# Values of the first group requested ahead of the weights, second-layer weights in another row order, probabilities as 24 rows

## The chip, the cores and the metric

The kernel runs on one core of a Trainium2 chip. The time is the device time of one launch in microseconds (us). A core has a matrix engine (PE, with its weight loads PEld), a vector engine (DVE), an activation engine (ACT), GpSimd (POOL) and a sync engine (SP). DMA requests are issued by SP, ACT and POOL; only POOL's may change the type on the way (fp32 in memory, fp16 on the chip).

## The reference

Attention over 4 batches, 8 heads, 768 positions and 64 values a head. Heads 0, 2 and 6 see all earlier positions ("retrieval" heads); the other five see the first 4 positions and a window of 64. The result, as a matrix x of 3072 rows by 512, goes through four experts, each with two layers, and their outputs are summed with normalised probabilities:

```
scores = scale * np.matmul(q, k.transpose(0, 1, 3, 2))
scores = np.where(mask[None, :, :, :], scores, -1000000000.0)
a = np.exp(scores - np.max(scores, axis=-1, keepdims=True))
a = a / (np.sum(a, axis=-1, keepdims=True) + 1e-09)
attn_out = np.matmul(a, v)
...
p = domain_probs / (domain_probs.sum(-1, keepdims=True) + 1e-09)
for e in range(E):
    h = np.maximum(x @ w1[e], 0.0)
    out += p[:, e:e + 1] * (h @ w2[e])
```

w1[e] is 512 by 1024 and w2[e] is 1024 by 512, in fp32: 2 MB each, 16 MB for the four experts.

## The kernel before

The order of instructions on every engine is fixed when the program is built: the code is emitted in the order in which each engine is to run it, attention interleaved with the experts by planned durations.

Attention works on groups of 384 positions (8 groups, two a batch). Group 0 comes first and has PE for itself. Its queries and keys come as fp32 by SP's and ACT's queues (L384, L397), and its values by POOL's queue, which casts them to fp16 (`load_v`, L287): head 0 at L406, heads 2, 1, 3, 4, 6 at L477, heads 5 and 7 at L479. Between these two stands `load_w1(0)` (L478), the first-layer weights of expert 0, in two requests of 64 partitions; `load_w2(0)` (L480) follows. Streaming heads land in `vS`, retrieval heads in `vR`. Masks are added on PE from `bC` and `bS`, which POOL builds (L423 to L449); the third column block of `bS` is a copy made by ACT (L812). A matmul on the tile `warm` (L416, `warm_up`) computes nothing that is used; it is put in where PE would wait. For the values of heads 3, 4, 5, 6 and 7 there are 4, 4, 6, 8 and 10 of them (L748, L680). Values are multiplied at L691 (retrieval) and L755 (streaming); the normalised result goes through ACT (L773, L783), DVE (L778) or a transpose (L732, L736) into `xT`.

The first four tiles of 128 rows go through the experts plainly (`plain_steps`, L956): first for three tiles, expert by expert, then for the fourth. Layer one is L969 (weights `w1sb` stationary, `xT` moving, 384 columns, or 128 columns for the fourth tile), the relu is ACT L982 into `hA`, layer two is L990 (`hA` stationary, `w2sb` moving, 512 columns), and DVE adds up (L1002, L1006). DVE also forms sums of the second-layer weights (`weight_sums`, L940) into `tsb`. The other 20 tiles go in pairs (`pair_steps`, L1068): layer one at L1081 (256 columns, `w1sb` stationary) and layer two at L1114 as seven products of half size.

The row order of the weights matters here. A hidden row of the second layer has to sit on the partition on which its hidden unit sits in `hA`. `load_w2` (L331) puts row 8*fi + fo of w2 on partition fi: eight neighbouring rows, 16 KB in one stretch of memory for each partition. The hidden units of one block of 128 are then every eighth column of w1, and `w1_tile` (L327) reads the stationary operand with a step of eight fp16 elements.

POOL's queue of requests is paced by hand with `landed` (L487): a copy of one element that waits for a request to land. In order: `load_w1(1)`, wait for w1(0), keys and queries of group 1, wait for w2(0), `load_w2(1)`, wait for the queries, retrieval values of group 1, `load_w1(2)`, wait for w2(1), and so on (L497 to L512).

The probabilities are read once at L398 as `[128, 24, 4]` in pieces of 16 bytes, normalised on DVE in `small_things` (L884 to L894) and, at the start of expert 1, transposed on PE (`turn_probs`, L900, L902), copied by DVE (L906) and written to a table `p_rows` in memory (L907), from which `load_probs` (L1028) reads two rows at a time for the pairs. The first four tiles use the normalised tile `p_sb` directly (L999).

Of the kernel before, what the change touches and what calls it, by code (L numbers as in the profile page):

```python
# [17 lines left out]
def kernel(  # L18
# [34 lines left out]
    P = 128  # L53
# [83 lines left out]
    mW = mS.rearrange("p t x -> p (t x)")[:, 0 : (WT + 2) * WQ].rearrange(  # L137
        "p (t x) -> p t x", t=WT + 2
    )
    probs = pers.tile([P, NTILE, E], FP32, name="probs")  # L140
    psums = pers.tile([P, NTILE], FP32, name="psums")
    rprobs = pers.tile([P, NTILE], FP32, name="rprobs")
    p_sb = pers.tile([P, NTILE, E], FP32, name="p_sb")

# [177 lines left out]
                in_=x[u, :, :, f0:f1],  # L324
            )

    def w1_tile(e, ct, ft):  # L327

        return w1sb[:, e * DMP + ct, :].rearrange("p (x f) -> p f x", f=FTP)[:, ft, :]

    def load_w2(e):  # L331
        gp.dma_start(
            out=w2sb[:, e * FTP : (e + 1) * FTP, :],
            in_=moe_w2[e].rearrange("(fi fo) d -> fi fo d", fi=P),
        )


# [38 lines left out]

    q32, k32 = rows32(0), rows32(1)
    v_s32 = early[0:NS, 0:1024].bitcast(FP32).rearrange("p (h d) -> p h d", h=H)
    for h in range(H):
        if h == 2:  # L380
            nc.sync.dma_start(
                out=v_s32, in_=v[0, :, 0:NS, :].rearrange("h r d -> r h d")
            )
        nc.sync.dma_start(out=k32[:, :, h, :], in_=rows_of(k, 0, h, 0))  # L384
        if h == HP:

            nc.scalar.add_instruction(
                mybir.InstLoadActFuncSet(
                    name=nc.get_next_instruction_name(),
                    engine=ENG.Activation,  # L390
                    act_func_set_id=[x.name for x in SETS].index(
                        "natural_log_exp_and_others"
                    ),
                )
            )
        eng = nc.scalar if h < HP else nc.sync
        eng.dma_start(out=q32[:, :, h, :], in_=rows_of(q, 0, h, 0))  # L397
    nc.sync.dma_start(  # L398
        out=probs, in_=moe_domain_probs.rearrange("(t p) e -> p t e", p=P)
    )  # L400
    nc.vector.memset(warm.bitcast(FP32), 0.0)
    nc.vector.memset(eps, 1e-9)
# [71 lines left out]

    mask_c(bC, 0.0, -60000.0)
    mask_s(bS[:, 0:2, :], 2, 0.0, -60000.0)
    load_v(0, 0, [2, 1, 3, 4, 6])  # L477
    load_w1(0, 0, F)  # L478
    load_v(0, 0, [5, 7])  # L479
    load_w2(0)  # L480
    zero(gp, kR[0][:, 1, :, :, :])
    zero(gp, kS[:, 1, :, :, :])
# [41 lines left out]
    def attention(b, c):  # L524
# [151 lines left out]
        def values_r(h):  # L676

            ps = pV.tile([P, 512], FP32, name="pV", bufs=2)
            if first:
                warm_up(ps, {6: 8}.get(h, 0), 256)  # L680
            ps = ps[:, 0 : 3 * (D + 2)].rearrange("p (j x) -> p j x", j=3)
            work = []
            for j in range(3):
                for es, parts in es_of[h]:
                    for t, o, q0, nq in parts:
                        x = j * P - q0
                        if 0 <= x < nq:
                            work.append((j, t, es[:, o + x : o + x + P]))
            ns = 0
            for n, (j, t, lhsT) in enumerate(work):  # L690
                nc.tensor.matmul(  # L691
                    out=ps[:, j, 0 : D + 1],
                    lhsT=lhsT,
                    rhs=vR[i][:, t, RH.index(h), 0 : D + 1],
                    start=(n == 0),
                    stop=(n == len(work) - 1),
                    skip_group_check=True,
                )
                ns += mm_ns(D + 1)
                if ns > 200 and n < len(work) - 1:  # L700
                    yield ns
                    ns = 0
            rs = att.tile([P, 3, 1], FP32, name="rs", bufs=2)
            nc.vector.tensor_scalar(
                out=rs, in0=ps[:, :, D : D + 1], scalar1=1e-9, scalar2=None,
                op0=ALU.add,
            )
            nc.vector.reciprocal(out=rs, in_=rs)
            ct, u = PLACE[h]
            x = x_pair if ct else x_one  # L710
            nc.vector.tensor_tensor(
                out=x[:, :, half(u)], in0=ps[:, :, 0:D],
                in1=rs.to_broadcast([P, 3, D]), op=ALU.mult,
            )
            yield ns
            if h != 2 and not first:
                nc.sync.dma_start(
                    out=xT[g][:, ct, :].rearrange("p (j x) -> p j x", j=3),
                    in_=x.rearrange("p j x -> p (j x)"),
                    transpose=True,  # L720
                )
# [16 lines left out]
        def values(h):  # L738
            if RETR[h]:
                yield from values_r(h)  # L740
                return
            ct, u = PLACE[h]
            if first and u == 1:
                ps = pO.tile([P, 512], FP32, name="pO", bufs=2)
            else:
                ps = pV.tile([P, 512], FP32, name="pV", bufs=2)
            if first:
                warm_up(ps, {3: 4, 4: 4, 5: 6, 7: 10}.get(h, 0), 256)  # L748
            work = []
            for es, parts in es_of[h]:  # L750
                for t, o, q0, nq in parts:
                    work.append((es, t, o, q0, nq))
            ns = 0
            for n, (es, t, o, q0, nq) in enumerate(work):
                nc.tensor.matmul(  # L755
                    out=ps[:, q0 : q0 + nq],
                    lhsT=v_tile(b, c, h, t),
                    rhs=es[:, o : o + nq],
                    start=(n == 0),
                    stop=(n == len(work) - 1),  # L760
                    skip_group_check=True,
                )
                ns += mm_ns(nq)
                if ns > 300 and n < len(work) - 1:
                    yield ns
                    ns = 0

            r, o = half(u), half(1 - u)
            pair = first and h in (3, 4)
            if not pair or u == 0:  # L770
                rc_of[0] = att.tile([P, CH], FP32, name="rc", bufs=2)
            rc = rc_of[0]
            nc.scalar.activation(  # L773
                out=rc[r, :], in_=ps[o, 0:CH], func=AF.Ln, bias=eps[o, :]
            )

            def scale(r=r, ps=ps):
                nc.vector.tensor_tensor(  # L778
                    out=xT[g][r, ct, :], in0=ps[r, 0:CH], in1=rc[r, :], op=ALU.mult
                )  # L780

            if not pair:
                nc.scalar.activation(out=rc[r, :], in_=rc[r, :], func=AF.Exp, scale=-1.0)  # L783
                later(scale, g)
            elif u == 0:
                scale_of[0] = scale
            else:
                nc.scalar.activation(out=rc, in_=rc, func=AF.Exp, scale=-1.0)
                later(scale_of[0], g)
                later(scale, g)  # L790

            yield ns + (600.0 if g == 1 else 400.0)
# [14 lines left out]
        if first:  # L807
# [1 line left out]
            yield from scores(0)  # L809
            sink_row(1)  # L810
            sink_row(3)
            nc.scalar.copy(out=bS[:, 2, :], in_=bS[:, 1, :])  # L812
            yield from transposes(1)
            yield from scores(2)
            sink_row(4)
# [59 lines left out]
    def small_things():  # L875
        def to_mask(x, bias):
# [4 lines left out]
        to_mask(mC, bC)  # L881
        to_mask(mS[:, 0:3, :], bS)
        to_mask(mS[:, 3, :], bS[:, 2, :])
        nc.vector.tensor_reduce(  # L884
            out=psums, in_=probs, axis=mybir.AxisListType.X, op=ALU.add
        )
        nc.vector.tensor_scalar(
            out=psums, in0=psums, scalar1=1e-9, scalar2=None, op0=ALU.add
        )
        nc.vector.reciprocal(out=rprobs, in_=psums)  # L890
        for e in range(E):
            nc.vector.tensor_tensor(
                out=p_sb[:, :, e], in0=probs[:, :, e], in1=rprobs, op=ALU.mult
            )  # L894


    p_rows = tc.dram_tile([NTILE, E * P], FP32, name="p_rows")
    pair0 = 4

    def turn_probs():  # L900
        ps = bank()
        nc.tensor.transpose(  # L902
            ps[0 : NTILE * E, 0:P], p_sb.rearrange("p t e -> p (t e)"), ident32
        )
        pT = moe.tile([P, P], FP32, name="pT", tag="sums", bufs=1)[0 : NTILE * E, :]
        nc.vector.tensor_copy(out=pT, in_=ps[0 : NTILE * E, 0:P])  # L906
        nc.sync.dma_start(out=p_rows.rearrange("t (e x) -> (t e) x", e=E), in_=pT)  # L907


    behind = []  # L910
# [45 lines left out]
    def plain_steps(nt0, tiles, e, tokens, n0):  # L956
# [6 lines left out]
        for f0 in [0, *range(ahead, FTP)]:  # L963
# [3 lines left out]
            def layer1(ft, n):  # L967
                ct = cts[n]
                nc.tensor.matmul(  # L969
                    out=pss[ft][:, 0:cols_n],  # L970
                    lhsT=w1_tile(e, ct, ft),
                    rhs=x[:, ct, :],
                    start=(n == 0),
                    stop=(n == DMP - 1),
# [93 lines left out]
    def pair_steps(nt0, nxt):  # L1068

        sums = [lambda: last_weight_sum(E - 1)] if nt0 == pair0 else []  # L1070
        for e in range(E):
# [5 lines left out]
            for f0 in range(0, FTP, 2):  # L1077
                ps = bank()
                for f in range(2):
                    for ct in range(DMP):  # L1080
                        nc.tensor.matmul(  # L1081
                            out=ps[:, f * PC : (f + 1) * PC],
                            lhsT=w1_tile(e, ct, f0 + f),
                            rhs=xs[:, ct, :],
                            start=(ct == 0),
                            stop=(ct == DMP - 1),
# [98 lines left out]
    def moe_steps():  # L1185
        for e in range(E):
            if e == 1:
                turn_probs()
            yield from plain_steps(0, 3, e, lambda: xT[0], (e % 2) * FTP * CH)
            weight_sums(e)  # L1190
        for e in range(E):
# [121 lines left out]
```

## Time and profile before

| | us |
|---|---|
| median of 4 runs | 386.55 (386.44 to 387.88) |
| the profiled execution | 386.31 |
| its span, first to last instruction | 384.6 |
| PE busy | 376.5 (98%) |
| PEld busy | 334.5 (87%) |
| DVE busy | 235.3 (61%) |
| ACT busy | 234.4 (61%) |
| POOL busy | 110.5 (29%) |

The busy shares are averages over the whole span; the kernel has stages with different limits. Group 0's attention fills about the first 22.6 us, the plain steps reach to about 91 us, the pairs fill the rest. In the lists, xN is a count of instructions, "idle" is the time in which the engine had nothing to run just before, and an arrow names what ended it. A line of the chain gives start, length, engine, tile and line of the work that the end waited for.

### The profile page before, as it was taken

Reading aid. Unit: us, or ns where it says so; the run is one execution under the profiler, and the core shown is the slowest. Engines: PE = TensorE matmul, PEld = TensorE weight load, DVE = VectorE, ACT = ScalarE, POOL = GpSimd, SP = SyncE. Lnnn points to the kernel's source line nnn. Section 1 sums busy time; section 2 is a strip of 40 time slices with the busy share of each in tenths; the row PEclk is TensorE's granted clock in tenths of the full one; section 3 lists DMA queues with packets and bytes.
Section 4 is the critical chain, followed back from the end, with each engine's and each line's share of the span. In section 5 each row is a group of like instructions: output and inputs, shape, how many; then the busy total and the mean of one; then the engine's idle time right before and its main releaser. Section 6 shows DMA issues by size and latency. Waiting matters only on the chain.

```text
span 384.6 us, 9369 instructions
## 1 busy us (share of the span) xinstructions
PE 376.5 (98%) x3814; PEld 334.5 (87%) x3814; DVE 235.3 (61%) x516; ACT 234.4 (61%) x476; POOL 110.5 (29%) x152
## 2 busy tenths in 40 slices
PE   7989999999999999999999999999999999999996
PEld 4776567678998998999998998999998999999995
DVE  6745787567766657766547566775556565355440
ACT  3863568657786876765765775764765684551630
POOL 8823534855138028213800118202100000000000
PEclk9999999999999999999999999999999999999999
DMA  8999999999499959965950669965510210110001
GB/s 165 164 208 204 185 185 185 129 175 151 71 132 128 127 96 96 145 125 48 141 78 16 113 116 76 145 129 41 80 56 13 68 57 2 56 55 30 29 0 56
DMA packets 123608, 39.19 MB, mean 102 GB/s; under 512 B 116232, under 2 KB 116780, under 8 KB 123052
## 3 DMA queue, kind: packets, MB, share of 16 engines
q0 software_dynamic: 83232, 19.01, 55.8%
q1 hardware_dynamic: 38732, 19.18, 22.4%
q8 instruction: 30, 0.49, 0.6%
q10 hardware_dynamic: 1600, 0.39, 0.5%
q14 instruction: 14, 0.11, 0.1%
HBM read 44.88 MB, written 6.34 MB: 133 GB/s over the span
## 4 chain that ended last, share of the span: by engine, by line
PE 92%; POOL 3%; DMA 2%; DVE 1%; ACT 1%; issue 0%; POOLq 0%; ACTq 0%
PE pA L1081 37%; PE pO L1114 32%; PE pA L969 7%; PE pO L990 7%; PE pA L643 5%; DMA vS<-in_v_dram 2%; PE pV L691 2%; PE pV L755 2%; POOL vR L291 1%; POOL vS L297 1%; ACT es L661 1%; POOL early L440 0%; POOL w1sb L322 0%; PE pO L416 0%; PE pV L545 0%
## 5 line engine op out<-in xcount | busy, mean ns | idle before, releaser
L1081 PE MATMUL pA<-xs,w1sb 128*128 128x256 f16 x1280 | 149.5, 274 | 0.0
L1081 PEld LDWEIGHTS <-w1sb 128*128 128x128 f16 x1280 | 140.1, 145 | 0.6 <-DVE xs L1047 0.3
L1090 ACT ACTIVATE hA<-pA 128x512 f16<-128x512 f32 x160 | 94.6, 597 | 40.3 <-PE pA L1081 37.3
L1114 PEld LDWEIGHTS <-hA 128*128 128x128 f16 x1120 | 106.6, 98 | 12.8
L661 ACT ACTIVATE es<-pA 128x384 f16<-128x384 f32 (+2 forms) x122 | 59.3, 510 | 31.9 <-PE pA L643 27.3
L1114 PE MATMUL pO<-w2sb,hA 128*128 128x256 f16 x640 | 77.8, 272 | 0.0
L293 POOL DMA_DIRECT2D vS<-in_v_dram x30 | 29.6, 988 | 126.2 <-PE pV L755 125.2
L1047 DVE TENSOR_TENSOR xs<-xT,pB 128x1024 f16<-128x1024 f16 (+1 forms) x52 | 49.6, 972 | 20.2 <-PE pA L1081 20.2
L1114 PE MATMUL pO<-tsb,hA 128*128 128x256 f16 x480 | 58.6, 272 | 0.0
L938 DVE TENSOR_TENSOR hA<-hA 128x1024 f16<-128x1024 f16 (+1 forms) x80 | 41.9, 553 | 1.1
L778 DVE TENSOR_TENSOR xT<-pV,rc 64x384 f16<-64x384 f32 x37 | 20.6, 556 | 26.2 <-ACT rc L783 24.1
L982 ACT ACTIVATE hA<-pA 128x384 f16<-128x384 f32 (+1 forms) x64 | 22.8, 386 | 20.8 <-PE pA L969 18.1
L969 PE MATMUL pA<-xT,w1sb 128*128 128x384 f16 (+1 forms) x256 | 32.8, 277 | 0.1
L990 PE MATMUL pO<-w2sb,hA 128*128 128x512 f16 x128 | 30.5, 379 | 0.0
L969 PEld LDWEIGHTS <-w1sb 128*128 128x128 f16 x256 | 26.2, 146 | 3.5 <-issue 0.3
L1055 DVE TENSOR_TENSOR hA<-hA 128x512 f16<-128x512 f16 (+1 forms) x30 | 15.3, 511 | 19.3 <-ACT hA L1090 19.3
L773 ACT ACTIVATE rc<-pV,eps 64x384 f32<-64x384 f32 x37 | 21.3, 576 | 8.9 <-PE pV L755 7.7
L1135 DVE TENSOR_TENSOR o<-pO,s 128x256 f32<-128x256 f32 x30 | 12.7, 423 | 20.6 <-PE pO L1114 15.3
L643 PE MATMUL pA<-qT,kR 128*128 128x384 f16 (+2 forms) x120 | 23.3, 278 | 0.8 <-ACT qT L554 0.4
L1132 ACT COPY s<-pO 128x256 f32<-128x256 f32 x30 | 11.2, 372 | 18.1 <-PE pO L1114 17.3
L990 PEld LDWEIGHTS <-hA 128*128 128x128 f16 x128 | 11.9, 98 | 11.7
L291 POOL DMA_DIRECT2D vR<-in_v_dram x24 | 19.0, 808 | 5.6 <-DMA w2sb<-in_moe_w_dram 4.0
(115 smaller groups left out, 329.6 us busy)
## 6 DMA issues: line engine op xcount, KB each, us to landing
pB<-p_rows SPq DMA_DIRECT2D x10, 512.0 KB, 3.4
out_dram<-o SPq DMA_DIRECT2D x19, 256.0 KB, 4.5
w1sb<-in_moe_w_dram POOLq DMA_DIRECT2D x8, 512.0 KB, 10.1
w2sb<-in_moe_w_dram POOLq DMA_DIRECT2D x4, 1024.0 KB, 13.3
vS<-in_v_dram POOLq DMA_DIRECT2D x30, 112.0 KB, 3.6
k_rows<-in_k_dram POOLq DMA_DIRECT2D x18, 128.0 KB, 4.2
q<-in_q_dram POOLq DMA_DIRECT2D x18, 128.0 KB, 5.4
vR<-in_v_dram POOLq DMA_DIRECT2D x24, 48.0 KB, 5.4
```

The lines of the kernel that those rows point to most:

```text
L291: gp.dma_start(out=t[:, :, 0:D], in_=rows_of(v, b, h, c))
L293: gp.dma_start(out=t[:, :, own_v(h)], in_=windows_of(v, b, h, c))
L643: nc.tensor.matmul(out=ps[:, o : o + nq], lhsT=key_tile(b, c, h, t), rhs=qTs[b, c][:, hp, q0 : q0 + nq], start=(n == 0 or not first), stop ...
L661: nc.scalar.activation(out=es[:, 0:cols], in_=ps[:, 0:cols], func=AF.Exp, scale=SC)
L938: nc.vector.tensor_tensor(out=out, in0=a, in1=b, op=ALU.subtract)
L969: nc.tensor.matmul(out=pss[ft][:, 0:cols_n], lhsT=w1_tile(e, ct, ft), rhs=x[:, ct, :], start=(n == 0), stop=(n == DMP - 1),)
L982: nc.scalar.activation(out=hs[:, ft, :], in_=ps[:, 0:cols_n], func=AF.Relu)
L990: nc.tensor.matmul(out=ps_o, lhsT=hs[:, ft, j * P : (j + 1) * P], rhs=w2sb[:, e * FTP + ft, :], start=(ft == 0), stop=(ft == FTP - 1),)
L1047: nc.vector.tensor_tensor(out=o, in0=xin, in1=pb.to_broadcast([P, DMP, n, P]), op=ALU.mult)
L1081: nc.tensor.matmul(out=ps[:, f * PC : (f + 1) * PC], lhsT=w1_tile(e, ct, f0 + f), rhs=xs[:, ct, :], start=(ct == 0), stop=(ct == DMP - 1),)
L1090: nc.scalar.activation(out=blocks[:, b0 : b0 + 2, k0 : k0 + 2, :].rearrange("p t f x -> p f t x"), in_=ps.rearrange("p (f t x) -> p f t x" ...
L1114: nc.tensor.matmul(out=ps, lhsT=a[:, k, :], rhs=b(k), start=(first and k == 0), stop=(k == KT - 1), skip_group_check=not first,)
```

## The change

- `load_w2` puts row 128*fo + fi on partition fi: eight stretches of 2 KB for each partition in place of one of 16 KB. `w1_tile` is gone; L969 and L1081 read 128 neighbouring columns of `w1sb`.
- Values of group 0: heads 2 and 6 are requested as fp32 by SP's queue, behind the keys of heads 6 and 7, into a part of `tsb` that is not yet in use, and POOL copies them into `vR` as fp16 (`cast_v`). POOL requests heads 1, 3, 4, 5 and 7 in a row, ahead of `load_w1(0)`; `cast_v(2)` stands before `load_w1(0)` and `cast_v(6)` between it and `load_w2(0)`.
- The copy into the third block of `bS` moves from ACT to POOL, ahead of these requests.
- The dummy matmuls ahead of the values of heads 3, 4, 5, 6 and 7 are 3, 3, 4, 6 and 3 (before 4, 4, 6, 8 and 10).
- The probabilities are read twice: the first 512 rows as `[128, 4, 4]` in pieces of 16 bytes, for the plain steps, and all 3072 as 24 rows of 2 KB. The 24 rows are normalised on DVE at the start of expert 1 (`prob_rows`) and written to `p_rows` from there. The transpose on PE and its copy are gone.

```diff
     def load_w2(e):
-            in_=moe_w2[e].rearrange("(fi fo) d -> fi fo d", fi=P),
+            in_=moe_w2[e].rearrange("(fo fi) d -> fi fo d", fi=P),
...
-                    lhsT=w1_tile(e, ct, ft),
+                    lhsT=w1sb[:, e * DMP + ct, ft * P : (ft + 1) * P],
...
-                            lhsT=w1_tile(e, ct, f0 + f),
+                            lhsT=w1sb[:, e * DMP + ct, (f0 + f) * P : (f0 + f + 1) * P],
...
+    v32 = {
+        h: tsb[:, n, 0:2, :].rearrange("p k x -> p (k x)")[:, 0 : 6 * D].bitcast(FP32)
+        for n, h in enumerate((2, 6))
+    }
+    v32 = {h: x.rearrange("p (j d) -> p j d", j=3) for h, x in v32.items()}
+
+    def cast_v(h):
+        gp.tensor_copy(out=v_tiles(0, 0, h)[:, :, 0:D], in_=v32[h])
...
         nc.sync.dma_start(out=k32[:, :, h, :], in_=rows_of(k, 0, h, 0))
+        if h in (6, 7):
+            r = {6: 2, 7: 6}[h]
+            nc.sync.dma_start(out=v32[r], in_=rows_of(v, 0, r, 0))
...
     nc.sync.dma_start(
-        out=probs, in_=moe_domain_probs.rearrange("(t p) e -> p t e", p=P)
+        out=probs,
+        in_=moe_domain_probs[0 : NPL * P, :].rearrange("(t p) e -> p t e", p=P),
+    )
+    nc.sync.dma_start(
+        out=p_in.rearrange("t x e -> t (x e)"),
+        in_=moe_domain_probs.rearrange("(t x) e -> t (x e)", x=P),
     )
...
-    load_v(0, 0, [2, 1, 3, 4, 6])
+    gp.tensor_copy(out=bS[:, 2, :], in_=bS[:, 1, :])
+    load_v(0, 0, [1, 3, 4, 5, 7])
+    cast_v(2)
     load_w1(0, 0, F)
-    load_v(0, 0, [5, 7])
+    cast_v(6)
     load_w2(0)
...
-                warm_up(ps, {6: 8}.get(h, 0), 256)
+                warm_up(ps, {6: 6}.get(h, 0), 256)
...
-                warm_up(ps, {3: 4, 4: 4, 5: 6, 7: 10}.get(h, 0), 256)
+                warm_up(ps, {3: 3, 4: 3, 5: 4, 7: 3}.get(h, 0), 256)
...
-            nc.scalar.copy(out=bS[:, 2, :], in_=bS[:, 1, :])
...
+    def normalise(x, sums, out):
+        nc.vector.tensor_reduce(out=sums, in_=x, axis=mybir.AxisListType.X, op=ALU.add)
+        nc.vector.tensor_scalar(
+            out=sums, in0=sums, scalar1=1e-9, scalar2=None, op0=ALU.add
+        )
+        nc.vector.reciprocal(out=sums, in_=sums)
         for e in range(E):
             nc.vector.tensor_tensor(
-                out=p_sb[:, :, e], in0=probs[:, :, e], in1=rprobs, op=ALU.mult
+                out=out[:, :, e], in0=x[:, :, e], in1=sums, op=ALU.mult
             )
...
-    def turn_probs():
-        ps = bank()
-        nc.tensor.transpose(
-            ps[0 : NTILE * E, 0:P], p_sb.rearrange("p t e -> p (t e)"), ident32
-        )
-        pT = moe.tile([P, P], FP32, name="pT", tag="sums", bufs=1)[0 : NTILE * E, :]
-        nc.vector.tensor_copy(out=pT, in_=ps[0 : NTILE * E, 0:P])
-        nc.sync.dma_start(out=p_rows.rearrange("t (e x) -> (t e) x", e=E), in_=pT)
+    def prob_rows():
+        normalise(p_in, r_rows, p_out.rearrange("t e x -> t x e"))
+        nc.sync.dma_start(out=p_rows.rearrange("t (e x) -> t e x", e=E), in_=p_out)
```

More of the change, by code (lines that the diff above doesn't have):

```diff
@@ L139 @@
     )
[L140 to L143, printed above, removed]
+    NPL = 4
+    probs = pers.tile([P, NPL, E], FP32, name="probs")
+    psums = pers.tile([P, NPL], FP32, name="psums")
+    p_sb = pers.tile([P, NPL, E], FP32, name="p_sb")
+    p_all = moe.tile([P, 2 * E * P], FP32, name="p_all", tag="o", bufs=1)
+    p_in = p_all[0:NTILE, 0 : E * P].rearrange("t (x e) -> t x e", e=E)
+    p_out = p_all[0:NTILE, E * P : 2 * E * P].rearrange("t (e x) -> t e x", e=E)
+    r_rows = moe.tile([P, P], FP32, name="r_rows", tag="sums", bufs=1)[0:NTILE, :]
     kT = pers.tile([P, HP, P + CH], FP16, name="kT")
@@ L325, in load_w1 @@
             )
-    def w1_tile(e, ct, ft):
-        return w1sb[:, e * DMP + ct, :].rearrange("p (x f) -> p f x", f=FTP)[:, ft, :]
     def load_w2(e):
@@ L883, in small_things @@
         to_mask(mS[:, 3, :], bS[:, 2, :])
-        nc.vector.tensor_reduce(
-            out=psums, in_=probs, axis=mybir.AxisListType.X, op=ALU.add
-        )
-        nc.vector.tensor_scalar(
-            out=psums, in0=psums, scalar1=1e-9, scalar2=None, op0=ALU.add
-        )
-        nc.vector.reciprocal(out=rprobs, in_=psums)
+        normalise(probs, psums, p_sb)
+    def normalise(x, sums, out):
+        nc.vector.tensor_reduce(out=sums, in_=x, axis=mybir.AxisListType.X, op=ALU.add)
+        nc.vector.tensor_scalar(
+            out=sums, in0=sums, scalar1=1e-9, scalar2=None, op0=ALU.add
+        )
+        nc.vector.reciprocal(out=sums, in_=sums)
         for e in range(E):
             nc.vector.tensor_tensor(
-                out=p_sb[:, :, e], in0=probs[:, :, e], in1=rprobs, op=ALU.mult
+                out=out[:, :, e], in0=x[:, :, e], in1=sums, op=ALU.mult
             )
     p_rows = tc.dram_tile([NTILE, E * P], FP32, name="p_rows")
-    pair0 = 4
-    def turn_probs():
-        ps = bank()
-        nc.tensor.transpose(
-            ps[0 : NTILE * E, 0:P], p_sb.rearrange("p t e -> p (t e)"), ident32
-        )
-        pT = moe.tile([P, P], FP32, name="pT", tag="sums", bufs=1)[0 : NTILE * E, :]
-        nc.vector.tensor_copy(out=pT, in_=ps[0 : NTILE * E, 0:P])
-        nc.sync.dma_start(out=p_rows.rearrange("t (e x) -> (t e) x", e=E), in_=pT)
+    pair0 = NPL
+    def prob_rows():
+        normalise(p_in, r_rows, p_out.rearrange("t e x -> t x e"))
+        nc.sync.dma_start(out=p_rows.rearrange("t (e x) -> t e x", e=E), in_=p_out)
     behind = []
@@ L1187, in moe_steps @@
             if e == 1:
-                turn_probs()
+                prob_rows()
             yield from plain_steps(0, 3, e, lambda: xT[0], (e % 2) * FTP * CH)
```

## The prediction

> **What bounds the kernel now.** I read the chain of waits by engine first, then the costliest groups, then the chain in order of time, then the timelines of POOL, PE and DVE around the weights of expert 1.
>
> ```profile
> PE 92%; POOL 3%; DMA 2%; DVE 1%; ACT 1%; issue 0%; POOLq 0%; ACTq 0%
> L1081 PEld LDWEIGHTS <-w1sb 128*128 128x128 f16 x1280 | 140.1, 145 | 0.6 <-DVE xs L1047 0.3
> L1114 PEld LDWEIGHTS <-hA 128*128 128x128 f16 x1120 | 106.6, 98 | 12.8
> DMA  8999999999499959965950669965510210110001
> ```
>
> PE sets the end for 92% of the span. A weight load from the stepped `w1sb` takes 145 ns, one from packed `hA` 98 ns, for the same 128x128 form. The DMA row is full up to about 100 us (slices of 9.6 us): early on, a transfer lands when those ahead of it are through.
>
> The rest of the chain, POOL and DMA, lies in the first 23 us:
>
> ```profile
> 11.54 9.23 DMA vS<-in_v_dram
> 20.77 0.05 issue
> 20.82 0.42 PE pO L755 x4
> 21.24 0.17 PE pV L732 x3
> 21.41 1.09 PE pO L416 x10
> 22.50 0.25 PE pO L755 x4
> 22.75 2.26 PE pA L969 x13
> ```
>
> PE waits at 20.8 for the values of head 5, requested behind 2 MB of w1(0); ten dummies and head 7 follow, then expert 0. Later the chain is nothing but PE:
>
> ```profile
> 75.88 1.97 PE pA L969 x32
> ...
> 161.52 2.66 PE pA L1081 x24
> 167.20 1.79 PE pA L1081 x16
> 174.07 2.62 PE pO L1114 x24
> 180.72 1.75 PE pO L1114 x16
> ```
>
> Each of these pieces of L1081 and L1114 follows a small attention piece. The L1081 pieces are 0.04 longer: after short matmuls one stepped load isn't hidden. With 128 columns (L969 at 75.88) every matmul pays: 1.97/32 = 61.6 ns.
>
> Last, how close the weights are to their use:
>
> ```profile
> 12.87 0.59 POOL L332 DMA_DIRECT2D w2sb<-in_moe_w_dram  x1
> 26.10 0.56 POOL L332 DMA_DIRECT2D w2sb<-in_moe_w_dram  x1 [0.29 <-issue]
> 39.55 0.18 POOL L489 COPY seen<-w2sb 1x1 f16<-1x1 f16 x1 [0.65 <-DMA w2sb<-in_moe_w_dram]
> ...
> 39.55 1.03 PE L990 MATMUL pO<-w2sb,hA 128*128 128x512 f16 x4
> ...
> 37.21 0.81 DVE L554 CAST qT<-pV 128x384 f16<-128x384 f32 x1 [0.64 <-PE pV L545]
> ```
>
> w2(1), issued at 26.10, took 13.3 to land (39.4); POOL sees it at 39.55, the moment when PE needs it. There is no margin. Other margins, from issue plus landing time: w2(0) 25.5 against a first use at 28.2; w1(1) 30.7 against 33.5; w1(3) 63.3 against 64.1; w2(3) 68.0 against 70.3.
>
> **Packed weight loads (w1).** The starts of PE's matmuls give the spacing. L1081 to L1081: 109 ns in 1,184 cases, 139 to 149 in 36. L1114 to L1114, with packed weights: none of 1,044 above 115. So 36 x 0.037 = 1.3 us goes. The 128-column L969 come at 61.6 ns; warm matmuls show columns/2.4 + 2.5 (109, 163 and 216 ns for 256, 384 and 512), so 55.8 when packed: 128 x 5.8 ns = 0.7. The 384-column L969 show some ten gaps 20 ns too long: 0.2. Sum -2.2, on PE, the path. Bounds: 0 if the stepped load isn't the cause; -2.4. ACT's relus don't take it back: eight of 0.28 in that stage are 2.2 against 1.8 + 1.7 of PE per expert.
> The Trainium skill ("TensorE: Matmul & The Clock Gate", Weight-path perf modes) says that the fast weight load works for chunks "packed or strided", with steps up to 1,024 elements, and the section on LDWEIGHTS counts columns alone. By that a step of eight costs nothing and the sum below would be 2.2 higher, 387.2; the rows of 145 against 98 disagree.
>
> **The front.** Heads 5 and 7 are now requested at about 9.1 and 9.8 (copy of bS 0.3, then 0.68 each by L297's rows from 6.76). The three requests issued from 7.5 to 9.6 landed 3.7 to 5.5 later, so they are there by about 15; the wait at 20.8 goes. ACT loses L812 (0.32), which PE waits for at 9.41 (0.40 idle): -0.25 there. Then PE reaches head 5 after 4 dummies at 18.7 + 0.44 = 19.1 in place of 20.8. The pair's transpose has to wait for DVE (L711 ended at 20.2): 20.0. Three dummies in place of ten, head 7 at 20.5 in place of 22.3. L969 then waits for head 5's xT some 0.4. Front: -1.7. L902: -0.1.
> What could eat it: SP's two more requests (0.53 each) delay q of head 7 from 8.0 to 9.1; at the usual 3.4 it lands at 12.5, when PE wants it (12.6). POOL's cast has no row; it lies between the one-element COPY (0.18) and L440 (1.46); nearest is the 128x128 fp32 select (0.29), so 0.4. Behind it wait w1(0) (from 10.3 to about 11) and values(2) at 11.3. w1(0) is needed at 20.7, landed at 20.2 before.
>
> **The transfers up to w2(1).** From landings: w2(1) follows the queries (21.37 + 13.4 = 34.8): 4.6 us for 1 MB written, in pieces of 8 KB. w1(1) follows w2(0): 25.5 to 30.7, 5.2 us per MB in pieces of 2 KB. Keys and queries of group 1: 30.7 to 34.8 for 0.75 MB, 5.5 us per MB in pieces of 384 bytes. The new w2 comes in pieces of 1 KB as written: between the last two, 5.3, so +0.7 each. Bounds: 0, and the 128-byte rows of group 2 (7.8 us per MB): +3.2. I take 0.7, the rows next to it.
> Probabilities: 3,072 pieces of 16 bytes in the two windows 10:12 and 12:14, where the profile shows 97 and 146 GB/s against some 210 around: 1.7 us lost at most, less the part of the small v pieces; 0 to 1.7, taken 1.0. The 512 pieces and 24 rows that remain: 0.2. Heads 2 and 6 as 256-byte fp32 writes: +0.2. So -0.6.
> w2(1) lands at -0.6 + 2 x 0.7 = +0.8, about 40.2. PE would be there at 37.7 and waits 2.5 us: all of the front is given back, and 0.7 more is lost. While it waits, layer two of expert 1 and behind it group 1's transposes stand. Next: w1(3) -0.6 + 2.1 = +1.5 (64.8 against 64.1 + 0.7), w2(3) +2.2 (70.2 against 71.0): just in time.
> The longest idle of PE after its start is 1.1 now, with a full granted clock in all slices; 2.5 would be new.
> The same page (The HAM clock gate) drops the clock after about 3.4 us of idleness; that would add an estimated 1.7 (3.4 us at half clock). 2.5 is below it; by the rule nothing is added.
>
> **DVE.** The 24-row normalisation, from the 24-element rows stretched to 512 and 128 elements: reduce 0.24 to 0.68, add 0.29, reciprocal 0.18 for 3 and 0.30 for 24 elements, so 0.9 for 128, four products 1.0: 2.8 in place of L906's 0.28 (bounds 1.2 to 3.3). It stands ahead of L554 at 37.2. DVE has it done at 37.4; the two transposes' copies (2.4) then end at 39.85 in place of 40.0: covered by PE's wait for w2(1). Without that wait, it is what is late: the second keys (PE at 40.7) come 0.85 early, no more. SP's p_rows write waits for it, the sink rows behind (L315) are used from 58 on.
>
> **Sum.** 386.3 - 2.2 (w1) - 1.8 (front) + 2.5 (wait for w2(1)) = 384.8. The median stood 0.2 above the profiled execution: 385.0.
>
> **Rivals.**
> - *The front is kept in part.* If pieces of w2 cost nothing and the probabilities free 1.7, w2(1) lands early and DVE's 0.85 is the limit: 386.5 - 2.2 - 0.9 = 383.5. For it: the 5.2 and 5.5 differ little. Against it: every measured size below 8 KB is slower.
> - *Slower: small pieces of w2 hold up experts 1 to 3.* At 1.75 each w2(1) lands +2.9, w1(3) +4.6 against a margin of 0.8 (PE +3.8), w2(3) +6.4 (PE +4.2); less 2.2 is +2.0: 388.5. It breaks even at 1.4 each and passes 0.3% at about 1.6. For it: no load with this shape is in the trace, and margins are nil. Against it: 2 KB and 384 bytes stand on both sides at 5.2 and 5.5.
> - *w1's step isn't what costs.* Then packed loads don't shorten the 36 gaps, and the sum is 387.2 or, with a front partly kept, 386.
>
> **Chances.** Forecast 0.42, kept front 0.22, slower 0.28, no effect of w1 0.08. About 0.3% (1.2 us) is what this measurement can tell from no change. Of the forecast's own range, 384.0 to 386.2, some 0.30 lies below 385.4 and 0.12 above: faster 0.52, same 0.20, slower 0.28. Range 383.0 to 388.4, from the bounds of the first two rivals.
>
> **What would show it.** Loads of w1sb at 98 ns; 128-column L969 at 56 ns; no L1081 gap near 145. L969 first at about 20.8. PE idle at 37 to 40 released by w2sb's DMA, which lands near 40. DVE 2.8 at 35. Wrong if PE runs through 37 to 40 without a wait, if w2 takes over 6 us per MB, or if the gaps stay.

## The result, and the profile after

The kernel after takes 385.54 us (median of 54 runs, 384.23 to 389.45), the kernel before 386.70 (78 runs, 385.86 to 390.43). The ratio is 0.9964, 95% interval 0.9953 to 0.9974: 1.2 us faster by the medians, 1.4 by the ratio (0.0036 of 386.7); 385.0 was predicted. The profiled execution took 387.69 (span 384.9), more than the median: 2.75 us of it lie outside the span, against a median of 1.7 over the 54 runs; the rest is seen below.

The first lines are from the page of the kernel after: the granted clock in 40 slices of 9.6 us, the chain of waits by engine, and three of the costliest groups (busy time and mean duration; idle time before them and what ended it). L1096 is the old L1081, L1129 the old L1114, L1005 the old L990, L984 the old L969.

```profile
PEclk9999899999999999999999999999999999999999
...
PE 86%; DMA 7%; POOL 3%; DVE 2%; ACT 1%; issue 1%; POOLq 0%; ACTq 0%
...
L1096 PEld LDWEIGHTS <-w1sb 128*128 128x128 f16 x1280 | 122.4, 98 | 14.5 <-DVE xs L1062 0.4
...
L1129 PEld LDWEIGHTS <-hA 128*128 128x128 f16 x1120 | 106.6, 98 | 12.9
...
L1005 PE MATMUL pO<-w2sb,hA 128*128 128x512 f16 x128 | 31.8, 391 | 2.2 <-DMA w2sb<-in_moe_w_dram 2.2
```

The load from `w1sb` now takes what the one from `hA` takes: 98 ns in place of 145. But 7% of the chain is a DMA of `w2sb`, which no line of the chain before had, and one slice lacks its full clock. The chain in order of time (start, length, what) shows where:

```profile
8.52 1.99 POOL vS L302 x3
10.51 0.35 POOL vR L387
10.86 1.17 POOL w1sb L327 x2
12.03 0.27 POOL vR L387
12.29 14.72 DMA w2sb<-in_moe_w_dram
...
27.59 13.17 DMA w2sb<-in_moe_w_dram
...
40.81 1.20 PE pO L1005 x4
...
42.79 2.92 PE pO L1005 x8
...
78.44 1.79 PE pA L984 x32
```

Up to 40.8 the end depends on POOL's requests and on two loads in a row: w2(0), for whose landing POOL waits before it requests w2(1), and w2(1) itself. Group 0's attention isn't in this chain any more. PE's own timeline (start, busy, line, operation, count, idle before it) says the same:

```profile
37.09 1.47 PE L984 MATMUL pA<-xT,w1sb 128*128 128x384 f16 x8
40.81 1.20 PE L1005 MATMUL pO<-w2sb,hA 128*128 128x512 f16 x4 [2.25 <-DMA w2sb<-in_moe_w_dram]
...
42.73 2.99 PE L1005 MATMUL pO<-w2sb,hA 128*128 128x512 f16 x8
```

PE is through with layer one of expert 1 at 38.6 and stands 2.25 us. Then eight matmuls of layer two take 2.92 in the chain; the same eight took 1.83 in the chain before. The windows give the reason (window, its length, busy time and count of PE, PEld, DVE, ACT and POOL, then the granted clock, the DMA share and GB/s):

```profile
40.00:42.00 2.00, 1.19 (x6) 0.37 (x8) 0.57 (x1) 0.00 (x0) 0.81 (x2) 0.89 0.91 122
42.00:44.00 2.00, 2.00 (x17) 1.00 (x17) 1.45 (x3) 0.00 (x0) 2.00 (x4) 0.50 1.04 161
44.00:46.00 2.00, 2.00 (x11) 0.99 (x10) 1.53 (x2) 0.03 (x1) 1.62 (x3) 0.76 1.12 207
46.00:48.00 2.00, 1.82 (x15) 1.00 (x13) 1.09 (x3) 2.00 (x5) 0.18 (x1) 1.00 1.54 177
```

The clock was halved from 41.55 on, for 3.413 us by the trace's record of the clock. Against the kernel before, PE in this execution is 1.11 early at its first w2 matmul (27.06 against 28.17), 1.26 late at w2(1) (40.81 against 39.55), 2.56 late at the 128-column stage (78.44 against 75.88), and 0.3 late at the end. Behind the halved clock, at the first L663 (45.71 against 42.86 before), it is 2.85 late: 2.85 - 1.26 = 1.6 us are the clock. From 78 us to the end it makes up 2.3, where the packed loads work. Of the 54 executions ten have a mean granted clock of 0.9965 or less, with a median span of 384.65; the other 44 have 383.55. The profiled one is of the ten, so its 387.69 isn't the time to compare. That the other nine owe their clock to this wait isn't shown: of the 82 executions of the kernel before that stand beside the experiments, 12 have such a clock too (median span 386.5, the other 70 have 384.7), though in its trace PE never stands longer than 1.1 us after its start. No trace shows where those lose their clock.

DVE, in the same columns:

```profile
35.23 0.67 DVE L906 TENSOR_REDUCE r_rows<-p_all 24x128 f32<-24x512 f32 x1
35.93 0.21 DVE L907 TENSOR_SCALAR r_rows<-r_rows 24x128 f32<-24x128 f32 x1
36.18 0.94 DVE L910 RECIPROCAL r_rows<-r_rows 24x128 f32<-24x128 f32 x1
37.15 1.25 DVE L912 TENSOR_TENSOR p_all<-p_all,r_rows 24x128 f32<-24x128 f32 x4
38.33 0.77 DVE L574 CAST qT<-pV 128x384 f16<-128x384 f32 x1
```

The 24-row normalisation is 3.07 us, and the cast of the first transposed query waits for it, while PE waits for w2(1).

### The profile page after: what moved, and what is told of

Same layout as the page of the kernel before. It is cut to its first block, busy times and chain, and to the rows that moved or that the text cites. A ratio compares the mean times of both kernels' runs of the same rounds, so it can differ in the third digit from the quotient of the medians.

```text
span 384.9 us, 9353 instructions
## 1 busy us (share of the span) xinstructions
PE 374.1 (97%) x3800; PEld 310.2 (81%) x3800; DVE 237.7 (62%) x522; ACT 233.2 (61%) x475; POOL 109.9 (29%) x153
## 4 chain that ended last, share of the span: by engine, by line
PE 86%; DMA 7%; POOL 3%; DVE 2%; ACT 1%; issue 1%; POOLq 0%; ACTq 0%
PE pA L1096 35%; PE pO L1129 32%; DMA w2sb<-in_moe_w_dram 7%; PE pO L1005 6%; PE pA L663 5%; PE pA L984 4%; PE pV L711 2%; PE pV L775 2%; POOL vS L302 1%; ACT es L681 1%; DVE kS L282 0%; POOL early L458 0%; DVE hA L1021 0%; POOL w1sb L327 0%; DVE xs L1062 0%
## 5 line engine op out<-in xcount | busy, mean ns | idle before, releaser
L1096 PE MATMUL pA<-xs,w1sb 128*128 128x256 f16 x1280 | 148.0, 272 | 0.1
L1096 PEld LDWEIGHTS <-w1sb 128*128 128x128 f16 x1280 | 122.4, 98 | 14.5 <-DVE xs L1062 0.4
L1105 ACT ACTIVATE hA<-pA 128x512 f16<-128x512 f32 x160 | 94.3, 597 | 39.2 <-PE pA L1096 36.7
L1129 PEld LDWEIGHTS <-hA 128*128 128x128 f16 x1120 | 106.6, 98 | 12.9
L1129 PE MATMUL pO<-w2sb,hA 128*128 128x256 f16 x640 | 77.8, 272 | 0.0
L1129 PE MATMUL pO<-tsb,hA 128*128 128x256 f16 x480 | 58.6, 272 | 0.0
L1005 PE MATMUL pO<-w2sb,hA 128*128 128x512 f16 x128 | 31.8, 391 | 2.2 <-DMA w2sb<-in_moe_w_dram 2.2
L984 PE MATMUL pA<-xT,w1sb 128*128 128x384 f16 (+1 forms) x256 | 31.8, 272 | 0.4 <-DVE xT L798 0.3
L1070 DVE TENSOR_TENSOR hA<-hA 128x512 f16<-128x512 f16 (+1 forms) x30 | 15.3, 511 | 18.8 <-ACT hA L1105 18.5
L984 PEld LDWEIGHTS <-w1sb 128*128 128x128 f16 x256 | 19.3, 98 | 8.9 <-issue 0.8
L1005 PEld LDWEIGHTS <-hA 128*128 128x128 f16 x128 | 12.0, 100 | 15.4 <-DMA w2sb<-in_moe_w_dram 3.0
L663 PE MATMUL pA<-qT,kR 128*128 128x384 f16 (+2 forms) x120 | 23.3, 278 | 0.4 <-DVE kR L581 0.4
L803 ACT ACTIVATE rc<-rc 64x384 f32<-64x384 f32 x38 | 19.8, 521 | 1.2
```

The lines of the kernel that those rows point to most:

```text
L663: nc.tensor.matmul(out=ps[:, o : o + nq], lhsT=key_tile(b, c, h, t), rhs=qTs[b, c][:, hp, q0 : q0 + nq], start=(n == 0 or not first), stop ...
L984: nc.tensor.matmul(out=pss[ft][:, 0:cols_n], lhsT=w1sb[:, e * DMP + ct, ft * P : (ft + 1) * P], rhs=x[:, ct, :], start=(n == 0), stop=(n = ...
L1005: nc.tensor.matmul(out=ps_o, lhsT=hs[:, ft, j * P : (j + 1) * P], rhs=w2sb[:, e * FTP + ft, :], start=(ft == 0), stop=(ft == FTP - 1),)
L1096: nc.tensor.matmul(out=ps[:, f * PC : (f + 1) * PC], lhsT=w1sb[:, e * DMP + ct, (f0 + f) * P : (f0 + f + 1) * P], rhs=xs[:, ct, :], start= ...
L1105: nc.scalar.activation(out=blocks[:, b0 : b0 + 2, k0 : k0 + 2, :].rearrange("p t f x -> p f t x"), in_=ps.rearrange("p (f t x) -> p f t x" ...
L1129: nc.tensor.matmul(out=ps, lhsT=a[:, k, :], rhs=b(k), start=(first and k == 0), stop=(k == KT - 1), skip_group_check=not first,)
```

## Experiments

Each run stands beside runs of the kernel before on the same chip; "ratio" is to these, with its 95% interval.

### The weights alone, the front alone

e2 puts only the packed reading of w1 into the kernel before:

```diff
 def w1_tile(e, ct, ft):
-    return w1sb[:, e * DMP + ct, :].rearrange("p (x f) -> p f x", f=FTP)[:, ft, :]
+    return w1sb[:, e * DMP + ct, ft * P : (ft + 1) * P]
```

> The kernel before with layer one reading 128 neighbouring columns of w1sb, w2 left in its old row order; hidden units and rows of w2 then don't belong together, so the second layer computes another sum of the same size. Nothing else differs. Theory 'packed loads shorten PE's path by 2.2 us': loads of w1sb at 98 ns, 128-column layer one at 56 ns, no gaps near 145 ns in the pairs' first layer, and 386.7 - 2.2 = 384.5. Rival 'a stepped load is hidden anyway': loads of 98 ns and 386.7, no change. Rival 'group 1 or DVE takes part of it back': between 385.0 and 386.

Measured: 384.43, ratio 0.9937 (0.9916 to 0.9957): -2.2 by the medians (386.65 before), -2.4 by the ratio; the profiled spans are 382.5 and 384.6, -2.1. The theory holds: the step of eight elements cost what the long gaps and the 128-column spacing said. In its trace no spacing of two L1081 is left between 139 and 149 ns (1,226 of 1,228 are 115 or less), and the 128-column L969 come every 56 ns.

e4 adds the new row order of w2 to that, and nothing of the front:

```diff
-            in_=moe_w2[e].rearrange("(fi fo) d -> fi fo d", fi=P),
+            in_=moe_w2[e].rearrange("(fo fi) d -> fi fo d", fi=P),
```

> The kernel before with the new order of w2's rows and packed reads of w1, all else as before (values, probabilities, dummies). Theory of the sum: -2.2 from packed loads, w2(1) lands about 1.4 to 2 later than 39.4, PE at 39.6 waits 1.3 to 1.9: 386.7 - 2.2 + 1.6 = 386.1. The front of the change then brings only what lies between this and 385.5. Rival 'the front is what made the changed kernel faster': 386.7 or more here.

Measured: 385.44, ratio 0.9964 (0.9945 to 0.9983), the same as the whole change. PE's waits for w2(1) in e2 and in e4, one line of each timeline:

```profile
39.77 1.02 PE L990 MATMUL pO<-w2sb,hA 128*128 128x512 f16 x4 [0.23 <-DMA w2sb<-in_moe_w_dram]
```

```profile
39.95 1.02 PE L990 MATMUL pO<-w2sb,hA 128*128 128x512 f16 x4 [0.65 <-DMA w2sb<-in_moe_w_dram]
```

e5 is the kernel after with both weight orders put back (the two diffs above reversed, at L984 and L1096):

> The changed kernel with both orders of the weights undone (w2 in stretches of 16 KB, layer one reading every eighth column of w1sb): values, probabilities and dummies of the change alone. Theory 'the front is given back before the pairs, because the weights of expert 1 and DVE are late': PE starts the experts about 1.2 to 1.7 us earlier (near 21.2), waits at the second layer of expert 1 or behind DVE's row normalisation, and the time is that of the kernel before, 386.2 to 386.9. Rival 'the front is worth its 1.7 us, and it was the short pieces of w2 that hid it': 385.0 or less.

Measured: 387.02, ratio 1.0010 (0.9993 to 1.0028). The front alone brings nothing. Its PE timeline:

```profile
39.15 1.04 PE L1005 MATMUL pO<-w2sb,hA 128*128 128x512 f16 x4 [0.79 <-DMA w2sb<-in_moe_w_dram]
...
40.52 0.36 PE L565 MATMUL pV<-ident,k 128*64 128x128 f16 x6
```

The first L984 ran at 20.98 (22.59 before), w2(1) began at 39.15 (39.55 before), with a wait of 0.79 in front of it, and the second key transposes were at 40.52 against 40.70. Even with w2 in long stretches the gain of the front ends at w2(1).

### The wait for w2(1): its pieces, the clock, DVE

e3 is the kernel after with w2 in stretches of 16 KB again:

```diff
-            in_=moe_w2[e].rearrange("(fo fi) d -> fi fo d", fi=P),
+            in_=moe_w2[e].rearrange("(fi fo) d -> fi fo d", fi=P),
```

> The changed kernel with w2 loaded as before, 16 KB in one stretch for each partition, w1 still packed; hidden units and rows of w2 don't belong together, so the second layer computes another sum of the same size. Theory 'short pieces of w2 make w2(1) late': w2(0) takes about 4.6 us in place of 6.2, w2(1) lands near 39.0 in place of 40.8, PE waits about 0.5 us in place of 2.25, the granted clock stays at 1, and the time is 385.5 less 1.7 to 2.5: 383.0 to 383.8. Rival 'w2(1) is late because of what stands ahead of it in the queue, not by its pieces': it lands after 40.3 and the time is 385.0 or more.

Measured: 384.38, ratio 0.9938 (0.9916 to 0.9961). Its PE timeline:

```profile
39.08 1.04 PE L1005 MATMUL pO<-w2sb,hA 128*128 128x512 f16 x4 [0.40 <-DMA w2sb<-in_moe_w_dram]
...
40.91 0.36 PE L565 MATMUL pV<-ident,k 128*64 128x128 f16 x6 [0.51 <-DVE kS L597]
```

The wait falls from 2.25 to 0.40, and at once DVE, late by the normalisation, is what PE waits for. The gain on the kernel after is 1.2 us by the medians, 1.0 by the ratios, but the two intervals still touch.

e1 fills the wait with dummy matmuls, so that PE isn't idle:

```diff
             ps_o = pO.tile([P, DM], FP32, name="pO", bufs=2)
+            if e == 1 and nt == 0:
+                warm_up(ps_o, 9, 512)
```

> The changed kernel with nine dummy matmuls of 512 columns (9 x 0.216 = 1.9 us) on PE between layer one and layer two of expert 1, where PE idles 2.25 us for w2(1). Theory 'the clock': the idle wait lets the granted clock fall to half for 3.4 us in part of the executions, which costs about 1.7 us each time. Then w2(1) lands as before (40.8), the wait is filled, no granted clock below 1 stands in the trace after 5 us, the second layer of expert 1 runs at 0.86 us for four matmuls, and the median falls from 385.5 to about 385.0 (the spread above it shrinks). Rival 'the clock is rare or harmless, the spread is the landing of w2(1)': the median stays at 385.5 or rises by up to 0.3 where the dummies outlast the wait.

Measured: 384.99, ratio 0.9953 (0.9936 to 0.9970), 0.4 us below the kernel after by the ratio, with intervals that overlap: not to be told apart. In the profiled execution w2(1) landed as late as in the kernel after, at 40.88, and PE then ran at full clock:

```profile
38.86 2.11 PE L434 MATMUL pO<-early 128*128 128x512 f16 x9
40.92 1.02 PE L1007 MATMUL pO<-w2sb,hA 128*128 128x512 f16 x4
...
42.33 1.90 PE L1007 MATMUL pO<-w2sb,hA 128*128 128x512 f16 x8
```

e7 moves DVE's normalisation out of the way:

```diff
-            if e == 1:
+            if e == 0:
                 prob_rows()
```

> The changed kernel with the 24-row normalisation put on DVE right after the small tiles (near 24.5 us), where DVE idles 4.6 us, in place of just before group 1's copies. Theory 'DVE is covered by PE's wait for w2(1)': DVE's copies of group 1 start 2 us or more earlier, PE still waits for w2(1) until about 40, no change: 385.2 to 385.8. Rival 'DVE takes part in the loss': 384.9 or less.

Measured: 384.95, ratio 0.9968 (0.9943 to 0.9993): no change that can be told. As long as w2(1) is late, DVE is covered. Its timeline has a second use:

```profile
40.48 1.04 PE L1005 MATMUL pO<-w2sb,hA 128*128 128x512 f16 x4 [2.23 <-DMA w2sb<-in_moe_w_dram]
...
41.90 1.90 PE L1005 MATMUL pO<-w2sb,hA 128*128 128x512 f16 x8
```

PE stood 2.23 us, as long as in the kernel after, and this time the clock stayed full (1.90 for the eight matmuls, not 2.99). The record of the clock tells the two apart. In all fourteen traces its stretches, from the first full clock to the last whole one, are whole multiples of 3.413 us: 37.547, 3.413 and 341.333 in the kernel after, 378.879 in e7. Counted in such windows, the wait of the kernel after (38.56 to 40.81) lies in one, 38.13 to 41.55, and the next is at half clock; the wait of e7 (38.25 to 40.48) is divided at 39.93 into 1.68 and 0.55. Over all traces the seven windows with 2.16 us or more of idleness of PE were each followed by half a clock, and none with 1.85 or less.

e9 is e3 and e7 together:

> The changed kernel with w2 in stretches of 16 KB and packed reads of w1 (hidden units and rows of w2 don't belong together, so the second layer computes another sum of the same size), and the 24-row normalisation early on DVE. With the long stretches alone the second keys' transposes waited 0.51 us for DVE's copies behind the normalisation. Theory 'with w2 early DVE is what is late': that wait goes, nothing else takes its place before 45 us, and 384.4 falls to 383.7 to 384.0. Rival 'w2(1) holds PE anyway': 384.4, no change.

Measured: 384.18, ratio 0.9922 (0.9898 to 0.9946); DVE's wait was gone, but PE then stood 1.04 for w2(1), which landed at 39.26. 0.2 below e3, with intervals that overlap: inconclusive. e12 is e1 and e7 together:

> The kernel after with both small additions: nine dummy matmuls ahead of the second layer of expert 1 (e1_dummies) and the 24-row normalisation at the start of expert 0 (e7_rows_early). Theory (the landing of w2(1) sets this stage; the granted clock costs 1.6 us in some executions only): between 384.6 and 385.2, ratio 0.995 to 0.997, as each of them alone. Rival (DVE's normalisation and the clock each hold up PE behind the wait): the two gains add up, 384.2 or less, ratio 0.994 or below.

Measured: 385.18, ratio 0.9969 (0.9956 to 0.9983). The two don't add up. Why isn't shown, since in the profiled execution w2(1) landed at 39.63 already and the dummies outlasted it by 1.2 us:

```profile
38.90 2.11 PE L434 MATMUL pO<-early 128*128 128x512 f16 x9
40.84 1.03 PE L1007 MATMUL pO<-w2sb,hA 128*128 128x512 f16 x4
```

### w2(1) requested first

If the landing of w2(1) holds this stage, it has to be requested earlier. e6 puts it ahead of the keys and queries of group 1 and lets group 1's attention begin later:

```diff
     landed(w1_of(0))
+    load_w2(1)
     load_triples(k, k16, 0, 1)
-    load_triples(q, qt16, 0, 1)
     landed(w2_of(0))
-    load_w2(1)
+    load_triples(q, qt16, 0, 1)
     landed(qt16[0:1, 0, 0, 0:1])
...
-    plan = {1: (1.15 * UNIT, 3.5 * UNIT)}
+    plan = {1: (1.6 * UNIT, 3.5 * UNIT)}
```

> The changed kernel with w2(1) requested ahead of the keys and queries of group 1 (POOL's order of requests), and group 1's attention planned 0.45 of an expert's plain step later (1.6 in place of 1.15), so that its first transposes stand behind the first 12 matmuls of expert 1's second layer. Theory 'one load in the wrong place of the queue costs the front': w2(1) lands near 36, PE runs from layer one into layer two of expert 1 at about 38.6 without a wait, the transposes at 41 find their rows landed (about 40.7), and the time falls by what PE idled, 2 us, less up to 1 us where w1(2) becomes the next late load: 383.5 to 384.5. Rival 'all transfers up to group 1 have to be in anyway, the wait only moves to the next': 385.3 to 386.

Measured: 390.13, ratio 1.0080 (1.0053 to 1.0107): slower, against the theory. w2(1) landed at 36.08 and PE had no wait for it, but POOL and PE show what came instead:

```profile
40.35 0.18 POOL L509 COPY seen<-q 1x1 f16<-1x1 f16 x1 [12.58 <-DMA q<-in_q_dram]
...
43.03 1.27 POOL L327 DMA_DIRECT2D w1sb<-in_moe_w_dram  x2
```

```profile
52.55 1.44 PE L984 MATMUL pA<-xT,w1sb 128*128 128x384 f16 x4 [6.26 <-DMA w1sb<-in_moe_w_dram]
```

The wait for the queries, which land last in this order, held w1(2) back: issued at 43.03 in place of 38.52. When the queries were in, nothing else had been requested, and the transfers paused (7 and 5 GB/s in the two microseconds from 40 to 42). PE stood 6.26 us, and the clock was half for 6.827.

e10 keeps that order but paces w1(2) by w2(1):

```diff
     load_triples(q, qt16, 0, 1)
-    landed(qt16[0:1, 0, 0, 0:1])
     load_v(0, 1, RH)
-    load_w1(2, 0, F)
     landed(w2_of(1))
+    load_w1(2, 0, F)
+    landed(qt16[0:1, 0, 0, 0:1])
```

> The kernel after, with w2(1) requested ahead of the keys and queries of group 1 as in e6_w2_first, but w1(2) now waits only for w2(1), not for the queries: w1(2) stands behind the retrieval values and is issued near 37 instead of 43. Attention of group 1 begins at 1.6 units of the plan instead of 1.15. Theory (in e6 it was the pacing wait that cost, and the wait for w2(1) is what the kernel after still loses): w2(1) lands near 36, w1(2) near 47 to 48 as in the kernel after, PE has no idle above 1 us between 37 and 55, and the time is 383 to 384, ratio about 0.991. Rival (the bytes ahead of expert 2 decide, in whatever order): PE waits over 2 us for w1(2), the queries or the values between 40 and 55, and the time is 385.5 or more, ratio 0.997 or above.

Measured: 383.84 (383.37 to 385.13), ratio 0.9939 (0.9920 to 0.9959). This is the lowest median of all, below both kernels: 1.7 us below the kernel after by the medians, 1.0 by the ratios, whose intervals just touch. POOL and PE:

```profile
36.08 0.18 POOL L509 COPY seen<-w2sb 1x1 f16<-1x1 f16 x1 [7.16 <-DMA w2sb<-in_moe_w_dram]
36.52 1.26 POOL L327 DMA_DIRECT2D w1sb<-in_moe_w_dram  x2 [0.27 <-issue]
```

```profile
37.90 2.75 PE L1005 MATMUL pO<-w2sb,hA 128*128 128x512 f16 x12
...
44.29 0.36 PE L565 MATMUL pV<-ident,k 128*64 128x128 f16 x6 [0.95 <-DVE kS L597]
```

w1(2) landed at 45.78, and PE goes from layer one into layer two at 37.90 without a wait; what is left is 0.95 for DVE. Two more kernels part this gain. e13 is e10's requests and plan with the new weight orders but the old front; e14 is the kernel before with e10's requests and plan alone.

> The kernel before with the new order of both weights and with the requests and the plan of e10_w2_first_no_gap, but with the old front: values of heads 5 and 7 behind w1(0), probabilities in 3072 pieces, the old dummies. Theory (w2(1) takes back all that the front brings; once w2(1) comes early, an earlier front stays): e10's time plus most of the 1.7 of the front, 385.0 to 385.5, ratio about 0.997. Rival (the front brings nothing in itself, all of e10's gain is packed loads and the earlier w2(1)): as e10, 383.5 to 384.2, ratio 0.992 to 0.9945.

> The kernel before with nothing but the requests and the plan of e10_w2_first_no_gap. Theory (in the kernel before w2(1) came in the moment of its use, so an earlier one has nothing to take away): 386.0 to 386.8, ratio 0.998 to 1.002. Rival (the new order of requests and the later attention of group 1 are a gain by themselves, of some 2): 384.5 to 385, ratio about 0.995.

e14 measured 386.49, ratio 0.9993 (0.9978 to 1.0008): before the change w2(1) was in time, and asking for it earlier takes nothing away. e13 measured 384.32, ratio 0.9948 (0.9932 to 0.9963), between its two expectations: the front is worth 0.3 to 0.5 us here (by the ratios and by the medians; the intervals overlap), not 1.7. Its PE timeline:

```profile
22.47 5.75 PE L969 MATMUL pA<-xT,w1sb 128*128 128x384 f16 x32
...
38.55 2.75 PE L990 MATMUL pO<-w2sb,hA 128*128 128x512 f16 x12
```

38.55 against e10's 37.90 is 0.65, and the spans (382.6 and 381.8) differ by 0.8: what the front has gained by then now stays. That it is so little is the front itself. The start of the first w2 matmul in all profiled executions is 27.67 to 28.17 with the old front (five kernels, middle 28.06) and 26.91 to 27.73 with the new one (nine kernels, middle 27.35): 0.7 between the middles, with a scatter of the same size.

## Why the prediction held, and where it did not

- **Packed weight loads, -2.2: right.** 98 ns in place of 145; 32 matmuls of 128 columns in 1.79 us, 56 ns each (55.8 predicted); no spacing of L1096 between 139 and 149 ns, where the kernel before has some 36; e2 -2.2 by the medians, -2.4 by the ratio. The Trainium skill ("TensorE: Matmul & The Clock Gate", Weight-path perf modes), by which a step would cost nothing, doesn't hold for this step of eight fp16 elements.
- **The front, -1.7 before it is given back: too large.** The wait for head 5 did go (its values ran at 19.30 without a wait), and L984 began at 20.97 for a predicted 20.8. But behind the first two matmuls PE waits for DVE's `xT`, as the prediction named it, and 1.1 is left at the first w2 matmul of this execution, 0.7 between the middles of all. The sum isn't hurt: e5 shows that all of it goes at w2(1).
- **w2(1) lands at 40.2 and PE waits 2.5: right in place and nearly in size, wrong in its terms.** It landed at 40.76, 40.88, 40.43 and 39.63 in the kernels after, e1, e7 and e12, which ask for it alike, with waits of 2.25 and 2.23 where no dummies fill them. But the probabilities, put at -0.6, brought little to be seen: w1(0) landed at 20.84 (20.20 before); the middles of all profiled executions are 19.95 with the new front (nine, 19.45 to 21.90) and 20.18 with the old (five). And small pieces of w2 cost less than 0.7 each. The trace has sixteen completion marks for each request; from the middle mark of w1(1) to that of w2(1), the next in the queue there, it is 5.29 and 5.04 us in e10 and e13 (1-KB pieces) and 4.96 in e14 (8-KB pieces): 0.1 to 0.3. From the middle mark of w1(0) to that of w2(1), over two loads of w2, the ten kernels with the old order of requests show 19.3 to 20.3 with 1-KB pieces (five, middle 20.02) and 18.8 to 19.5 with 8-KB pieces (five, middle 19.34): 0.3 each. What moved the landing in the kernel after is the last mark: there the middle mark of w2(1) came at 38.47 and the last at 40.76; before, at 38.28 and 39.43. In e7 it was the middle one (39.17, last 40.43). So the prediction was right there partly by luck, by two errors that cancelled.
- **"by the rule nothing is added": the step that failed in the profiled execution.** The prediction read 2.5 us of idleness against the 3.4 of the same page (The HAM clock gate) and added nothing. 2.25 us were enough there, and 2.23 weren't in e7's: by the windows shown with e7, what counts is how much of one window of 3.413 us is idle, not the length of the wait alone. It cost 1.6 us there. A lower granted clock is in ten of 54 executions (19%), but in the kernel before in 12 of 82 (15%), so the comparison of the two kernels shows little of it, and filling the wait (e1) brought nothing that can be told.
- **DVE's normalisation, 2.8 and covered: right.** 3.07 measured. e3 shows the cover gone: PE waits 0.51 for DVE. e7 shows that with the cover on, moving it brings nothing.
- **w1(3) and w2(3), "just in time": better in the profiled execution.** They landed at 61.62 and 66.26, for 64.8 and 70.2 predicted, and PE had no wait. That this comes from the pieces isn't shown: in e1, with the same requests, they landed at 65.59 and 70.33, and PE waited 0.29 for w1(3).
- **Sum.** -2.2, and +0.7 for front and wait together, were to give 385.0. Measured by the ratios, -2.4 for the packed loads (e2) and +1.0 for the rest (0.0027 of 386.6), in all -1.4. The rival with a kept front failed, since w2(1) holds it back; the slower one, since a w2 in small pieces costs 0.1 to 0.3; the one without an effect of w1 by e2. The slower one would have broken even, by the prediction's own margins, at about 1.25 each (4 x 1.25 - 0.6 - 2.2 = 2.2) and not at the 1.4 that it names; both are far from 0.3.

What stays open: why the last of the sixteen marks comes so late. It is behind the middle one by 0.7 to 1.3 us for w2(1) in the kernels before, e2, e3 and e4, 1.3 in e7, 1.4 in e5, 0.6 in e12, 2.3 and 2.4 in the kernel after and e1, in one execution each. In the kernel after and in e1 the distance is there from w1(0) on (1.8 and 2.8) and is handed from request to request. At w1(0), ahead of which e7 and e12 ask for the same as the kernel after, it is 0.6 and 0.8 in these: so it differs between executions and isn't a fixed cost of these requests. The 24 packets of 2 KB of the new load of probabilities took 84 to 96 ns each in the kernel after, too little for it even with two on one engine. No run was made to test it. It isn't shown either that e4's 1.0 us above e2 comes from the small pieces alone: their profiled spans differ by 0.2, and the intervals overlap.

## What to carry to other kernels

An earlier start is worth only what the next due transfer leaves of it: look for the load with no margin (here w2(1), seen in the moment of its use), and ask for it earlier in the same change. When requests are reordered, move the waits that pace the queue along with them: the places of two waits, on the queries, which now land last, and on w2(1), are all that lies between e6's 390.13 us and e10's 383.84. Read stationary weights in neighbouring columns where the layout of the other operand can follow, and look at the spacing of short matmuls, not only at the mean, to see what it is worth.

## What the runs showed of the hardware

- The matrix engine's clock fell to half after 2.25 us of idleness in one execution and stayed full after 2.23 in another. By the record of the clock it is granted in windows of 3.413 us, and half clock followed where one window held 2.16 us or more of idleness (seven windows), not where it held 1.85 or less. Half clock lasted 3.413 us, and 6.827, twice that, after the 6.26 us of e6.
- A request counts as landed by its slowest part. The middle marks of w2(1) lie within 1.5 us over the kernels with the old order of requests (37.7 to 39.2), the last ones within 1.9 (39.03 to 40.88), but in another order.
- A stationary load with a step of eight fp16 elements takes 145 ns against 98, but behind 256-column matmuls it shows in some 36 gaps of 1,200 only.
